# Edge sums on one core: smaller requests in more places between the tiles, leftover list and piece places through TensorE, third part merged while the second is split

## The chip, the core and the metric

The kernel runs on one core of a Trainium2 chip. The engines are TensorE (PE, with its weight loads listed apart as PEld), VectorE (DVE), ScalarE (ACT), GpSimd (POOL) and SyncE (SP). Each works through its own queue in order. The metric is the device time of one execution in microseconds. "Before" was run three times. A profile is one further execution.

## The reference

```python
def reference(x, src, dst, deg_inv, w_self, w_neigh):
    N = x.shape[0]
    nsum = _segment_sum(x[src], dst, N)
    h_neigh = nsum * deg_inv[:, None]
    return x @ w_self + h_neigh @ w_neigh
```

There are 12,500 nodes with 64 features each and 800,000 edges whose source and destination are drawn at random. For every destination the features of its sources are summed, scaled and multiplied by a 64x64 matrix; the node's own features through another matrix are added. Almost all of the work lies in bringing 800,000 edges into an order in which the sums can be made.

## The kernel before

**The order.** Every edge becomes a 32-bit key: a bucket (a block of 164 destinations with a block of 128 sources) and the two places inside the blocks. Each of the 128 partitions sorts 6,250 keys on DVE. The buckets are then dealt out in three parts of 128 rows, with 29, 20 and 10 buckets a row. For each part the places of 16 pieces in the sorted runs are counted (`find_rows`, ACT), the pieces are fetched by POOL and merged by DVE (lengths `LENA`), the rows are split once more among 8 (`split_rows`) and merged to the end (`LENB`). Then 128 keys around each bucket are fetched, decoded and turned (`change`). The edges beyond 128 in a bucket are the leftovers: `leftovers` picks them from the list `top`, brings two, four or seven rows together in `many`, picks again into `ltop`, and turns that list so that each column `lk` holds 128 leftover edges.

**The places.** `swap` turns counts that lie one way across the partitions into places that lie the other way: DVE subtracts (`st` or `stb`), DVE multiplies with a mask into `swapa`, one TensorE matmul writes `stp`, and DVE adds a base into the places `ixa` or `ixb`. POOL fetches by these. `split_rows` is run in one go of the generator as far as its ACT passes go (L530 to L534, eight sign passes with sums), then DVE's `stb` (L536), `swapa` (L487), `ixb` (L492), and POOL's eight fetches (L544), one a tile.

**The node stage.** `nodes` runs over the buckets in tiles of 8, some 945 tiles. For each 28 buckets SP loads a slab `slb` (L892) and DVE makes two one-hot tables, `ohs` (L894) and `ohd` (L899). For each tile PE selects the sources into `ct` (L925, 8 matmuls), ACT copies `ct` to `xg` (L935), and PE adds to `acc` (L1005, 16 matmuls of 64 rows, as 2 per bucket). Leftovers are fetched by POOL in columns of 128 (`lx`, `pick`, L956), spread by DVE (`ohl`, `spread`, L965) and added by PE (L973). PSUM has three buffers under the tag "ct"; `stp`, `po` and `fps` use the same ones.

**What sets the order.** The loop of `sums_and_merge` issues, after each tile, pieces of the other work. Merging of the second and third part is dealt out by a budget: `PACE` nanoseconds of estimated DVE time are added for each tile, and merge instructions are issued while the budget is above zero. `later_parts` is the one list from which this budget draws: the rest of the second part's `LENA` merges, its split, its `LENB` merges, and then the same for the third part. While a split waits (`"wait", 1` for each fetch, `"wait", 6` at the end), nothing is drawn. `leftovers` runs beside it and says by `yield` how many tiles to let pass:

```python
queue = nc.gpsimd if part else nc.scalar
queue.dma_start(self.tops[part], ...); yield 3
nc.vector.memset(many[:chk], 0.0)
queue.dma_start(many[...], self.tops[part]...); yield 8
...  # picks by DVE
queue.dma_start(self.lt[part]..., top); yield 3
queue.dma_start(k.bitcast(F32), ...lt turned...); yield 8
```

For the first part these four transfers are issued by ACT, for the others by POOL; the turn is done by writing `ltop` to DRAM and reading it across. Once the third part is turned (`self.changed`), DVE takes every other copy of `ct` (L933). After the last leftover list `check` (L1087) adds up counters; its one matmul `fps` follows DVE's sum `one` at once, and DVE reads `fps` at once.

## Time and profile before

| what | value |
|---|---|
| three runs | 1911.93, 1916.02, 1918.82 us (median 1916.02) |
| the profiled execution | 1898.32 us, span 1896.5 us, mean TensorE clock 0.973 |
| DVE busy | 1749.0 us (92%) |
| ACT busy | 1116.9 us (59%) |
| PE busy | 956.3 us (50%) |
| POOL busy | 569.8 us (30%) |
| DMA in the node stage, share of the 16 engines | 0.7 to 0.9 |

A row of the windows view gives a stretch of the span, its length, the busy time of each engine with the number of instructions, the mean granted TensorE clock and the share of the DMA engines. A row of the timeline gives the start, the time, the engine, the line, the operation, tiles and shapes, the count, and in brackets how long the engine stood idle before it and what ended that. Instructions of one kind that follow each other are one row with a count. The node stage begins at about 838 us.

### The profile page before, as it was taken

The page shows a single profiled execution, that of the slowest core. Times are in us where ns is not written, and L with a number is a line of the kernel's source. Part 1 is how long each engine was busy: PE and PEld are TensorE (multiplying, and loading weights), DVE is VectorE, ACT ScalarE, POOL GpSimd, SP SyncE. Part 2 cuts the span into 40 slices and gives each one's busy share as a digit, 9 for nine tenths or more (in the row PEclk, how much of TensorE's full clock was granted, in tenths as well). Part 3 has the DMA queues.
Part 4 walks back from the last instruction along what each step waited for, and adds up shares of the span by engine and source line. Part 5 has one row for each costly group of instructions (what it writes and reads, how often), then busy time and mean ns, then how long its engine had stood idle before and what let it go on. Part 6 is the DMA issues. An engine that isn't in the chain of part 4 may idle for free.

```text
span 1896.5 us, 54072 instructions
## 1 busy us (share of the span) xinstructions
PE 956.3 (50%) x23320; PEld 848.7 (45%) x23320; DVE 1749.0 (92%) x1773; ACT 1116.9 (59%) x1565; POOL 569.8 (30%) x440
## 2 busy tenths in 40 slices
PE   0052000000000000027799999897888899889996
PEld 0042000000000000016688888776777788778885
DVE  8999999999998999987899999999997999888985
ACT  7281000204001004338799999899889899968885
POOL 2000000055411100713435443573515224441341
PEclk9999999999999999998899999999998999989998
DMA  4353000022001100248798998987797899778994
GB/s 154 70 133 70 0 0 0 37 66 61 14 8 50 31 0 37 63 146 251 221 276 253 287 267 282 283 261 225 197 288 228 271 263 300 250 199 285 274 275 116
DMA packets 185332, 307.83 MB, mean 162 GB/s; under 512 B 136185, under 2 KB 141859, under 8 KB 184444
## 3 DMA queue, kind: packets, MB, share of 16 engines
q1 hardware_dynamic: 98268, 275.33, 44.5%
q0 software_dynamic: 78240, 28.72, 9.1%
q8 instruction: 184, 3.01, 0.6%
q10 hardware_dynamic: 8576, 0.24, 0.3%
q14 instruction: 64, 0.52, 0.1%
HBM read 277.29 MB, written 26.48 MB: 160 GB/s over the span
## 4 chain that ended last, share of the span: by engine, by line
DVE 21%; PE 18%; DMA 10%; issue 6%; ACT 5%; SPq 4%; POOL 2%; DVEq 0%; ACTq 0%; POOLq 0%
PE ct L925 10%; DMA slb<-sl 8%; DVE u L317 7%; PE acc L1005 7%; SPq L892 4%; DVE ohd L899 4%; DVE ohs L894 3%; ACT xg L935 3%; DVE u L351 2%; DMA lk<-lt 1%; POOL u L544 1%; PE acc L973 1%; PE po L1072 1%; POOL lx L956 1%; DVE ohl L965 1%
## 5 line engine op out<-in xcount | busy, mean ns | idle before, releaser
L935 ACT ACTIVATE xg<-ct 128x1024 f16<-128x1024 f32 x915 | 857.4, 1090 | 111.4 <-PE ct L925 79.3
L925 PE MATMUL ct<-xh,ohs 128*128 128x128 f16 x7546 | 530.6, 224 | 43.2 <-DVE ohs L894 22.2
L925 PEld LDWEIGHTS <-ohs 128*128 128x128 f16 x7546 | 453.9, 100 | 73.9 <-issue 27.9
L317 DVE TENSOR_TENSOR u<-u 128x1512 f32<-128x1512 f32 (+49 forms) x316 | 426.6, 1366 | 10.2 <-ACT u L301 6.2
L1005 PE MATMUL acc<-ohd,xg 64*128 64x82 f16 x15092 | 396.5, 201 | 41.2 <-ACT xg L935 16.3
L1005 PEld LDWEIGHTS <-xg 64*128 64x128 f16 x15092 | 325.4, 96 | 99.7 <-issue 30.6
L956 POOL DMA_INDIRECT lx<-xt,ls x127 | 241.1, 1899 | 427.4 <-PE acc L973 392.8
L899 DVE TENSOR_TENSOR ohd<-iota,dlT 128x2296 f16<-128x2296 bf16 x270 | 363.1, 1345 | 0.1
L894 DVE TENSOR_SCALAR ohs<-slb,pidx 128x3584 f16<-128x3584 bf16 x270 | 316.6, 1172 | 46.5 <-PE ct L925 24.2
L490 PE MATMUL stp<-cx,swapa 128*128 128x16 f32 (+1 forms) x12 | 3.5, 366 | 465.0 <-DVE swapa L487 465.0
L490 PEld LDWEIGHTS stp<-cx,swapa 128*128 128x128 f32 x12 | 3.0, 312 | 465.8 <-issue 301.4
L249 DVE TENSOR_TENSOR a<-b 128x1040 f32<-128x1040 f32 (+41 forms) x130 | 194.8, 1540 | 4.9 <-ACT b L251 1.7
L249 DVE TENSOR_TENSOR b<-a 128x1040 f32<-128x1040 f32 (+46 forms) x150 | 194.7, 1347 | 3.4 <-DVE a L249 0.5
L517 POOL DMA_INDIRECT u<-d,ixa x48 | 71.3, 1486 | 404.2 <-DVE ixa L492 396.9
L301 ACT ACTIVATE u<-u 128x256 f32<-128x256 f32 (+14 forms) x60 | 33.1, 625 | 174.1 <-DVE u L305 138.4
L695 POOL DMA_INDIRECT v<-d,ix x59 | 76.4, 1295 | 177.7 <-DVE ix L706 142.1
L251 ACT ACTIVATE b<-a 128x2 f32<-128x2 f32 (+31 forms) x41 | 16.0, 405 | 184.8 <-DVE a L249 167.4
L765 PE MATMUL tr<-idb,l 128*128 128x128 bf16 x59 | 8.0, 275 | 216.8 <-ACT l L759 216.8
L1081 POOL DMA_DIRECT2D out<-o x27 | 97.8, 3751 | 61.9 <-ACT o L1075 61.6
L765 PEld LDWEIGHTS <-l 128*128 128x128 bf16 x59 | 4.7, 119 | 219.2 <-POOL pad L415 171.0
L251 ACT ACTIVATE a<-b 128x1 f32<-128x1 f32 (+24 forms) x34 | 8.6, 259 | 118.8 <-DVE b L249 114.2
L305 DVE TENSOR_TENSOR u<-u 128x2016 f32<-128x2016 f32 (+11 forms) x40 | 62.0, 1564 | 15.2 <-DMA u<-da,ixb 8.2
(149 smaller groups left out, 784.4 us busy)
## 6 DMA issues: line engine op xcount, KB each, us to landing
slb<-sl SPq DMA_DIRECT2D x1076, 224.0 KB
xt<-xh SPq DMA_DIRECT2D x1, 3136.0 KB
out<-o POOLq DMA_DIRECT2D x25, 123.0 KB
own<-os SPq DMA_DIRECT2D x12, 256.0 KB
out<-os SPq DMA_DIRECT2D x12, 256.0 KB
rd<-dst SPq DMA_DIRECT2D x4, 521.0 KB
rs<-src SPq DMA_DIRECT2D x4, 521.0 KB
lx<-xt,ls POOLq DMA_INDIRECT x127
```

The source lines that it names most:

```text
L249: nc.vector.tensor_tensor(view(dst, lo + sh, [[st, g], [1, l]]), x, y, op=op)
L317: nc.vector.tensor_tensor(to, at(cur, ln + lo, n), at(cur, lo + k, n), op=op)
L517: nc.gpsimd.indirect_dma_start(out=u[:, i * w:(i + 1) * w], out_offset=None, in_=src, in_offset=bass.IndirectOffsetOnAxis(ap=self.start[pa ...
L695: self.nc.gpsimd.indirect_dma_start(out=self.v[:, k].bitcast(F32), out_offset=None, in_=flat(self.d2[part], 128 * PITCH2[part]), in_offset ...
L892: nc.sync.dma_start(b[j::4], bass.AP(tensor=src.tensor, offset=src.offset, ap=[[0, 32], [1, n * 128]]))
L894: nc.vector.tensor_scalar(s.rearrange("p c s -> p (c s)"), b, self.pidx[:, :1], None, op0=OP.is_equal)
L899: nc.vector.tensor_tensor(d, self.iota[:, None].to_broadcast(wide), ix, op=OP.is_equal)
L925: nc.tensor.matmul(ct[:, i * 128:(i + 1) * 128], cols[i][0], self.xh[:, (b0 + i) % NB].rearrange("p a f -> p (a f)"), start=True, stop=True)
L935: nc.scalar.activation(xg[:, :cnt * 128], ct[:, :cnt * 128], AF.Copy)
L956: nc.gpsimd.indirect_dma_start(out=x, out_offset=None, in_=self.xt, in_offset=bass.IndirectOffsetOnAxis(ap=self.left[p][1][:, c:c + 1].bit ...
L1005: nc.tensor.matmul(acc[h][:, db % OCT * HN:(db % OCT + 1) * HN], xg[r, i * 128:(i + 1) * 128], d[r], start=db % OCT == 0 and sb == 0, stop ...
L1081: nc.gpsimd.dma_start(out, o[:n, at], accum_op=OP.add)
```

## The change

**The places.** The subtraction and the addition move into the matmuls: the picking table is made negative, the constants are added up on the host into one table, and a second matmul with the identity adds that table in PSUM. DVE only makes `swapa`; ACT writes the places. In the node stage the steps are issued further apart: two of the eight ACT passes a tile, 4 tiles of pause, `swapa`, 6 tiles, the matmuls, 1 tile, the copy by ACT, a fetch a tile, and 5 tiles.

**The leftover list.** `many` is filled by POOL straight from `top` in on-chip memory, one transfer for each of the 2, 4 or 7 rows brought together; its clearing is done by POOL. The turn is a TensorE transpose `ltp` in a PSUM buffer of the tag "ct", copied by ACT. The tables `tops` and `lt` in DRAM are gone.

**The order of merging.** A stack of merge lists takes the place of `later_parts`. When a part's first merges are done, its split is queued beside the leftovers (to begin 6 tiles later); during the second part's split the budget goes to the third part's `LENA` merges, which have a buffer `u3` of their own. The budget is 270 and 275 instead of 260 and 300. Five leftover columns are held instead of four, they are spread up to 80 buckets ahead instead of 32, and `check` pauses 7 tiles ahead of its matmul and 6 behind it.

```diff
-PACE = (0, 260, 300)
+PACE = (0, 270, 275)
...
+HELD = 5
...
-          q[:, None] % NSUP == sup[None], q[:, None] % SUP == row[None]]
+          -(q[:, None] % NSUP == sup[None]).astype(np.float32), -(q[:, None] % SUP == row[None]).astype(np.float32)]
-        cx += [(q[:, None] % SUP * NSUP + sup[None]) * WIDE[p], (q[:, None] // SUP * SUP + row[None]) * PITCHA[p],
-               -(t - np.uint32(1)).view(np.float32), np.tile([n + lo - 1 for lo, n in WIN.wb[p]], (128, 1))]
+        at = np.array([n + lo - 1 for lo, n in WIN.wb[p]])
+        cx += [(q[:, None] % SUP * NSUP + sup[None]) * WIDE[p] + add[NSUP * p + q // SUP][:, None],
+               (q[:, None] // SUP * SUP + row[None]) * PITCHA[p] + at[q % SUP][:, None],
+               -(t - np.uint32(1)).view(np.float32)]
...
-    def swap(self, st, mps, mask, shape, pick, n, base, name):
+    def swap(self, acc, mps, mask, shape, pick, n, table, name):
         nc = self.nc
         a = self.keep.tile([128, 128], F32, name="swapa")
         nc.vector.tensor_tensor(a.rearrange("p (a b) -> p a b", a=view3[1]), src,
                                 mask.rearrange("p (a b) -> p a b", a=view3[1]), op=OP.mult)
+        yield 6
         ps = mps.tile([128, n], F32, name="stp", tag="ct", bufs=3)
-        nc.tensor.matmul(ps, a, pick, start=True, stop=True)
+        nc.tensor.matmul(ps, a, pick, start=True, stop=False)
+        nc.tensor.matmul(ps, self.idf, table, start=False, stop=True)
+        yield 1
         ix = self.keep.tile([128, n], U32, name=name)
-        nc.vector.scalar_tensor_tensor(ix, ps, 0.0, base, op0=OP.max, op1=OP.add)
-        return ix
+        nc.scalar.activation(ix, ps, AF.Copy)
+        self.places = ix
...
-        st = l1.tile([128, NSUP], F32, name=f"st{part}")
-        nc.vector.tensor_tensor(st, self.c1[:, 1, c0:c0 + NSUP], acc, op=OP.subtract)
-        self.start.append(self.swap(st, mps, self.cx[:, :128], ((NSUP, 1), (SUP, 0)),
-                                    self.cx[:, 256:256 + NSUP], NSUP, self.table(part, 0), f"ixa{part}"))
+        for _ in self.swap(acc, mps, self.cx[:, :128], ((NSUP, 1), (SUP, 0)), self.cx[:, 256:256 + NSUP], NSUP,
+                           self.table(part, 0), f"ixa{part}"):
+            pass
+        self.start.append(self.places)
...
-            yield i
-        st = self.keep.tile([128, SUP], F32, name=f"stb{part}")
-        nc.vector.tensor_tensor(st, self.table(part, 3), acc, op=OP.subtract)
-        yield SUP
-        ix = self.swap(st, mps, self.cx[:, 128:256], ((NSUP, 0), (SUP, 1)),
-                       self.cx[:, 256 + NSUP:256 + NSUP + SUP], SUP, self.table(part, 1), f"ixb{part}")
-        yield SUP
+            if i % 2:
+                yield 1
+        yield 4
+        for wait in self.swap(acc, mps, self.cx[:, 128:256], ((NSUP, 0), (SUP, 1)),
+                              self.cx[:, 256 + NSUP:256 + NSUP + SUP], SUP, self.table(part, 1), f"ixb{part}"):
+            yield wait
+        ix = self.places
         for j in range(SUP):
             self.pause(1)
-            yield SUP
+            yield 1
+        yield 5
...
-        queue = nc.gpsimd if part else nc.scalar
-        queue.dma_start(self.tops[part], self.top.rearrange("p j i -> p (j i)"))
-        yield 3
         many = pool.tile([max(CHK), max(g * (9 * c + 1) for g, c in zip(GRP, PCS))], F32, name="many")
-        nc.vector.memset(many[:chk], 0.0)
+        nc.gpsimd.memset(many[:chk], 0.0)
         many = many[:chk, :grp * n].rearrange("p (b i) -> p b i", b=grp)
-        full, rest = divmod(128, grp)
-        queue.dma_start(many[:full, :, :cand], self.tops[part][:full * grp].rearrange("(a b) i -> a b i", b=grp))
-        if rest:
-            queue.dma_start(many[full:chk, :rest, :cand], self.tops[part][full * grp:].unsqueeze(0))
+        found = self.top.rearrange("p j i -> p (j i)")
+        for b in range(grp):
+            nc.gpsimd.dma_start(many[:len(range(b, 128, grp)), b, :cand], found[b::grp])
         yield 8
...
-        yield 2
-        queue.dma_start(self.lt[part].rearrange("a (j i) -> a j i", i=8), top)
-        yield 3
+        yield 6
+        ps = self.mps.tile([128, chk], F32, name="ltp", tag="ct", bufs=3)
+        nc.tensor.transpose(ps, top.rearrange("p j i -> p (j i)"), self.idf[:chk, :chk])
+        yield 1
         k = pool.tile([128, chk], I32, name="lk")
-        src = self.lt[part]
-        queue.dma_start(k.bitcast(F32), bass.AP(tensor=src.tensor, offset=src.offset, ap=[[1, 128], [128, chk]]))
-        yield 8
+        nc.scalar.activation(k.bitcast(F32), ps, AF.Copy)
+        yield 5
...
-            if self.picked == len(done) or len([u for u in uses if u[5]]) >= 4:
+            if self.picked == len(done) or len([u for u in uses if u[5]]) >= HELD:
-                x = u[5] = pool.tile([128, 128], FH, name="lx", bufs=4)
+                x = u[5] = pool.tile([128, 128], FH, name="lx", bufs=HELD)
-            u[7] = pool.tile([128, 2, OCT * HN], FH, name="ohl", bufs=4)
+            u[7] = pool.tile([128, 2, OCT * HN], FH, name="ohl", bufs=HELD)
-            for u in uses[:4]:
-                if u[5] and not u[7] and len(done) >= u[6] + 10 and b0 + 32 >= (u[4] - 1) * NB:
+            for u in uses[:HELD]:
+                if u[5] and not u[7] and len(done) >= u[6] + 10 and b0 + 80 >= (u[4] - 1) * NB:
                     spread(u)
...
         nc.vector.tensor_reduce(one, self.cnt, axis=mybir.AxisListType.X, op=OP.add)
+        yield 7
         ps = mps.tile([1, 1], F32, name="fps", tag="ct", bufs=3)
         nc.tensor.matmul(ps, one, ones, start=True, stop=True)
+        yield 6
         nc.vector.tensor_scalar(self.flag, ps, float(E + 128 * 64 * (4 * n - sum(KPRS))), None, op0=OP.not_equal)
...
-        for dt in merge:
-            yield "merge", dt
-        for part, (u, w, pong) in ((1, (u1, x, u1)), (2, (u2, u1, u2))):
-            if part == 2:
-                for dt in self.merge_runs(LENA[2], u2, u1, NSUP):
-                    yield "merge", dt
-            for i in self.split_rows(part, u, w, mps, self.nc.gpsimd):
-                if i >= SUP:
-                    yield "wait", 1
-            yield "wait", 6
-            for dt in self.merge_runs(LENB[part], w, pong, SUP):
-                yield "merge", dt
-            self.rows[part] = w
-            yield "done", part
...
-        lefts = {0: [self.leftovers(0), 2]}
+        self.mps = mps
+        side = [[self.leftovers(0), 0]]
-        later = self.later_parts(merge, x, u1, u2, mps)
-        until = 0
+        home = {1: (u1, x, u1), 2: (u2, u1, u2)}
+        todo = [(merge, None)]
+        given, checked = 0, False
+
+        def split(part, n):
+            u, w, pong = home[part]
+            for wait in self.split_rows(part, u, w, mps, self.nc.gpsimd):
+                yield wait
+            todo.append((self.merge_runs(LENB[part], w, pong, SUP), part))
+
...
-                            self.check(fin, mps)
+                            side.append([self.check(fin, mps), 0])
...
-                        lefts[part] = [self.leftovers(part), 0]
+                        side.append([self.leftovers(part), n + 3])
             t += PACE[min(merging, 2)]
-            while t > 0 and later:
+            while t > 0 and todo:
+                dt = next(todo[-1][0], None)
+                if dt is not None:
+                    t -= dt
+                    continue
+                rows = todo.pop()[1]
+                if rows:
+                    self.rows[rows] = home[rows][1]
+                    merging += 1
                 else:
-                    merging += 1
+                    given += 1
+                    assert given == 1 or merging == 2
+                    side.append([split(given, n), n + 6])
+                    if given == 1:
+                        todo.append((self.merge_runs(LENA[2], u2, u3, NSUP), None))
+            t = min(t, 0)
+        assert checked
+        for job, _ in side:
+            for _ in job:
+                pass
```

The lines of the changed kernel are shifted by a few (L925 is L924, L935 is L934, L894 is L893, L317 is L319, L305 is L307, L544 is L546).

The first place is ACT from the start of the node stage to the second part's split (`junkb` are the sign passes, `tops`, `many`, `lt` and `lk` the first part's leftover list). Before:

```order
L935 ACTIVATE xg<-ct 128x1024 x3
L833 DMA tops_68<-top_1457 128x171
L935 ACTIVATE xg<-ct 128x1024 x3
L839 DMA many<-tops_68 64x2x171
L935 ACTIVATE xg<-ct 128x1024 x10
L855 DMA lt_71<-ltop 64x128
L935 ACTIVATE xg<-ct 128x1024 x3
L859 DMA lk<-lt_71 128x64x1
L935 ACTIVATE xg<-ct 128x1024 x8
L532 ACTIVATE junkb,accb_2485<-u,cx 128x10
L532 ACTIVATE junkb,accb_2485<-u,cx 128x103
L532 ACTIVATE junkb,accb_2485<-u,cx 128x141
```

Now:

```order
L934 ACTIVATE xg<-ct 128x1024 x16
L858 ACTIVATE lk<-ltp 128x64
L934 ACTIVATE xg<-ct 128x1024 x16
L534 ACTIVATE junkb,accb_2652<-u,cx 128x9
L534 ACTIVATE junkb,accb_2652<-u,cx 128x103
L934 ACTIVATE xg<-ct 128x1024
L534 ACTIVATE junkb,accb_2652<-u,cx 128x141
L534 ACTIVATE junkb,accb_2652<-u,cx 128x170
L934 ACTIVATE xg<-ct 128x1024
L534 ACTIVATE junkb,accb_2652<-u,cx 128x194
L534 ACTIVATE junkb,accb_2652<-u,cx 128x213
```

ACT issues no transfer there any more, and between two of the sign passes stands a tile's copy.

The second place is DVE from the places of the second part's split to the first merge behind it (L305, or L307 now, with 4x368). Before:

```order
L492 SCALAR_TENSOR_TENSOR ixb_2543<-stp,cx 128x8
L894 TENSOR_SCALAR ohs<-slb,pidx 128x3584
L899 TENSOR_TENSOR ohd<-iota,dlT 128x2296
L894 TENSOR_SCALAR ohs<-slb,pidx 128x3584
L899 TENSOR_TENSOR ohd<-iota,dlT 128x2296
L894 TENSOR_SCALAR ohs<-slb,pidx 128x3584
L899 TENSOR_TENSOR ohd<-iota,dlT 128x2296
L965 TENSOR_SCALAR ohl<-wide,lp_2482 128x2x82
L894 TENSOR_SCALAR ohs<-slb,pidx 128x3584
L899 TENSOR_TENSOR ohd<-iota,dlT 128x2296
L965 TENSOR_SCALAR ohl<-wide,lp_2482 128x2x164
L305 TENSOR_TENSOR u<-u 128x4x368
```

Now, the last rows ahead of that merge, which stands 28 rows behind `swapa` in DVE's order (the rows `u<-u 128x8x...` are third-part merges):

```order
L893 TENSOR_SCALAR ohs<-slb,pidx 128x3584
L898 TENSOR_TENSOR ohd<-iota,dlT 128x2296
L319 TENSOR_TENSOR u<-u 128x8x100
L964 TENSOR_SCALAR ohl<-wide,lp_2296 128x2x164
L893 TENSOR_SCALAR ohs<-slb,pidx 128x3584
L898 TENSOR_TENSOR ohd<-iota,dlT 128x2296
L964 TENSOR_SCALAR ohl<-wide,lp_2296 128x2x82
L319 TENSOR_TENSOR u<-u 128x8x104
L964 TENSOR_SCALAR ohl<-wide,lp_2296 128x2x82
L893 TENSOR_SCALAR ohs<-slb,pidx 128x3584
L898 TENSOR_TENSOR ohd<-iota,dlT 128x2296
L307 TENSOR_TENSOR u<-u 128x4x368
```

Third-part merges now stand where only one-hot tables stood. Before the last third-part merge there are 192 `ohs` instructions in the one order and 197 in the other, of 270.

The third place is POOL at the second part's split (`da` is the store of its rows). Before:

```order
L527 DMA da_66<-u 128x2412
L956 DMA lx<-xt,ls_2467 128x128
L544 DMA u<-da_66,ixb_2543 128x368
L415 MEMSET pad 128x100
L544 DMA u<-da_66,ixb_2543 128x368
L415 MEMSET pad 128x100
L956 DMA lx<-xt,ls_2467 128x128
```

Now:

```order
L836 MEMSET many 64x574
L840 DMA many<-top_1451 64x171 x2
L955 DMA lx<-xt,ls_2281 128x128 x5
L529 DMA da_66<-u 128x2412
L955 DMA lx<-xt,ls_2281 128x128 x6
L546 DMA u<-da_66,ixb_3135 128x368
L415 MEMSET pad 128x100
L546 DMA u<-da_66,ixb_3135 128x368
```

Eleven leftover columns are fetched ahead of the split's fetches, one among them; before it was one ahead and three among them.

57 lines of the change are left out of this document (21 added, 36 removed).

## The prediction

> **What bounds it now.** I read the windows view by stretches of the node stage first, once for all engines and once for line L925 alone (its matmuls divided by 8 are tiles), then each engine's waits in the timeline.
>
> ```profile
> 838.00:950.00 112.00, 82.09 (x1960) 73.27 (x1961) 88.44 (x125) 83.03 (x106) 37.34 (x34) 0.88 0.81 248
> 950.00:1210.00 260.00, 243.75 (x6354) 217.39 (x6353) 247.72 (x239) 252.48 (x305) 113.98 (x48) 0.99 0.91 274
> 1210.00:1410.00 200.00, 164.27 (x4048) 144.51 (x4047) 196.18 (x295) 176.82 (x241) 95.52 (x55) 0.96 0.83 245
> 1410.00:1470.00 60.00, 51.59 (x1243) 46.19 (x1242) 43.47 (x49) 54.90 (x80) 29.93 (x26) 0.89 0.81 238
> 1470.00:1610.00 140.00, 129.35 (x3320) 114.84 (x3312) 137.01 (x158) 132.52 (x169) 46.18 (x26) 0.98 0.89 277
> 1610.00:1690.00 80.00, 63.38 (x1498) 55.97 (x1496) 67.31 (x120) 61.71 (x85) 33.90 (x22) 0.89 0.73 219
> ```
>
> ```profile
> 838.00:950.00 112.00, 49.53 (x654) 42.65 (x655) 0.88 0.81 248
> 950.00:1210.00 260.00, 142.31 (x2084) 120.95 (x2083) 0.99 0.91 274
> 1210.00:1410.00 200.00, 94.27 (x1310) 79.76 (x1309) 0.96 0.83 245
> 1410.00:1470.00 60.00, 30.16 (x411) 25.81 (x408) 0.89 0.81 238
> 1470.00:1610.00 140.00, 74.82 (x1080) 63.52 (x1080) 0.98 0.89 277
> 1610.00:1690.00 80.00, 37.17 (x492) 32.21 (x492) 0.89 0.73 219
> ```
>
> The second stretch is undisturbed: 2084/8 = 260.5 tiles in 260 us, 0.998 us each, with PE, DVE and ACT all at 94 to 97%. There is no single bound, and a tile will not get much cheaper. Against that price the others lose time: the first has 81.8 tiles in 112 us, 30 us too long; 1210 to 1410 has 163.8 in 200, 37 too long; 1410 to 1470 has 51.4 in 60, 9 too long; 1470 to 1610 has 135 in 140, 5 too long; 1610 to 1690 has 61.5 in 80, 19 too long. But 1210 to 1410, the largest, has DVE at 196.18 of 200: real work (the second part's counting and decoding), which the change leaves. The first and fourth stretches have DVE idle for 23.6 and 16.5 us. Those are waits, and they have names:
>
> ```profile
> 853.74 1.01 PE L925 MATMUL ct<-xh,ohs 128*128 128x128 f16 x8 [5.22 <-ACT xg L935]
> 854.68 1.28 PE L1005 MATMUL acc<-ohd,xg 64*128 64x82 f16 x32
> 860.34 0.80 PE L1005 MATMUL acc<-ohd,xg 64*128 64x82 f16 x32
> 883.70 0.57 PE L490 MATMUL stp<-cx,swapa 128*128 128x8 f32 x2 [9.57 <-DVE swapa L487]
> 909.76 0.29 PE L973 MATMUL acc<-ohl,lx 128*128 128x82 f16 x2 [9.49 <-DVE ohl L965]
> 1426.29 0.57 PE L490 MATMUL stp<-cx,swapa 128*128 128x8 f32 x2 [6.10 <-DVE swapa L487]
> 1452.88 1.13 PE L925 MATMUL ct<-xh,ohs 128*128 128x128 f16 x16 [2.10 <-DVE ohs L894]
> 1453.94 1.28 PE L1005 MATMUL acc<-ohd,xg 64*128 64x82 f16 x32
> 1680.49 0.19 PE L1097 MATMUL fps<-ones,one 128*1 128x1 f32 x2 [4.05 <-DVE one L1095]
> ```
>
> ```profile
> 852.67 3.77 ACT L935 ACTIVATE xg<-ct 128x1024 f16<-128x1024 f32 x4 [6.27 <-DVE many L836]
> 880.43 0.20 DVE L863 TENSOR_SCALAR ls<-lk 128x64 int32<-128x64 int32 x1 [4.43 <-DMA lk<-lt]
> 905.52 1.69 DVE L305 TENSOR_TENSOR u<-u 128x1472 f32<-128x1472 f32 x1 [8.19 <-DMA u<-da,ixb]
> 1425.65 0.17 DVE L536 TENSOR_TENSOR stb<-cx,accb 128x8 f32<-128x8 f32 x1 [5.85 <-ACT junkb L532]
> 1448.89 1.93 DVE L305 TENSOR_TENSOR u<-u 128x816 f32<-128x816 f32 x2 [6.35 <-issue]
> ```
>
> The first PE stall is ACT held in its queue by the transfer that waits for DVE's clearing of `many`. The second is DVE standing for `lk`, the list turned through DRAM, with `stb` and `swapa` queued behind it. The third is DVE standing for the split's fetches at the first merge, with the `ohl` that PE needs queued behind. At 1426 DVE waits for eight sign passes in a row.
>
> **Part by part.** *Places, ahead of the node stage.*
>
> ```profile
> 390.91 0.17 DVE L508 TENSOR_TENSOR st<-c,acc 128x16 f32<-128x16 f32 x1
> 391.12 0.29 DVE L487 TENSOR_TENSOR swapa<-st,cx 128x128 f32<-128x128 f32 x1
> 392.18 0.17 DVE L492 SCALAR_TENSOR_TENSOR ixa<-stp,cx 128x16 uint32<-128x16 f32 x1 [0.77 <-PE stp L490]
> 392.27 2.38 DVE L249 TENSOR_TENSOR b<-a 128x1038 f32<-128x1038 f32 x2
> ```
>
> From 390.91 to 392.27 DVE spends 1.36 us; only `swapa`'s 0.29 stays. There DVE is the bound (the sort goes straight on behind), so each swap gives 1.07. Four lie ahead of 838 us: **-4.3**. The two-pass `stp` matmul here becomes two matmuls, some 0.4 us more ahead of POOL's fetches, hidden because DVE has other merges.
>
> *First stretch.* The three stalls named are 5.2 + 9.6 + 9.5 = 24.3 us of PE, and DVE's idle time is 23.6. All three causes go: no transfer on ACT, no DRAM turn, and third-part merges for DVE while the split runs. What stays is DVE's own 88.44 us. At the undisturbed stretch's density (247.72/260 = 0.953) that is 92.8 us, so 112 - 92.8 = 19.2; I take off 2 for slab waits at the start: **-17**. Bounds: nothing if each stall is replaced, 24.3 if all of it counts.
>
> *Third part's split.* The 6.1 us stall goes, since ACT's passes come two a tile. The wait at 1448.89 for the fetches has a cause that stays: POOL.
>
> ```profile
> 1427.81 1.27 POOL L544 DMA_INDIRECT u<-da,ixb  x1 [9.32 <-DVE ixb L492]
> 1443.72 0.95 POOL L544 DMA_INDIRECT u<-da,ixb  x1 [0.17 <-issue]
> 891.47 1.05 POOL L415 MEMSET pad<- 128x100 f32 x1
> POOL lx L956 <- PE acc L973: 392.8, 82, 13.3
> ```
>
> From the first fetch to the merge took 1448.89 - 1427.81 = 21.1 us; the new order leaves 13 tiles, 13 us, with fewer `lx` among the fetches. Of the 9 us lost I take **-6**; bounds 0 and 9. In these 35 tiles DVE has no merges at all, so it runs ahead and a wait of some us is covered by its one-hot tables.
>
> *Budget.* From 1210 to 1610 DVE is at 98%, so 25 ns less merging a tile is 25 ns less time: 299 tiles x 0.025 = 7.5. In the second stretch 10 ns more, on engines at 95%: 260 x 0.010 = 2.6 back. The same merges last 5 slabs or 17.5 tiles longer, at the undisturbed price those tiles have anyway: **-4.9**, bounds +2.6 and -7.5.
>
> *Check and clearing.* PE's 4.05 at 1680.49 goes, because the matmul comes 7 tiles behind DVE's sum: **-4**. DVE's clearing of `many` and the smaller swaps: **-1**. The leftover columns spread earlier cost DVE the same and move no bound where DVE is full.
>
> *What it adds.* Five copies by ACT in the node stage; the nearest row is L726's small ACT copy:
>
> ```profile
> L726 ACT ACTIVATE ix<-acc,c 128x1 uint32<-128x1 f32 x30 | 12.2, 407 | 0.0
> L839 POOL DMA_DIRECT2D many<-tops x2: 800/1122/1445, 1326.2 to 1650.2; - x2
> ```
>
> 5 x 0.41 = 2.0. `ltp`, `stp` and `fps` each keep one of three "ct" buffers for 1 to 6 tiles; with two left PE's fill still overlaps ACT's copy, so I take 1. POOL gets 13 transfers of `many` at 0.8 to 1.45 us: for the third part 7, 5.6 to 10.2 us, against a pause of 8 tiles. No cover lost if the lower, 2 us of DVE if the upper. Together **+3**, bounds +1 and +6.
>
> Sum: -4.3 - 17 - 6 - 4.9 - 4 - 1 + 3 = **-34.2 us** on the profiled execution's 1898.3, 1864.1. The runs' median lies 17.7 above that execution, so the forecast for the median is 1916.0 - 34.2 = **1882 us**.
>
> One rule speaks against clearing `many` on POOL: the Trainium skill (SBUF — State Buffer, Who interferes with whom) says that a GpSimd instruction and a DVE instruction in a two-port mode block each other for the whole instruction. The trace agrees that they meet: the 0.20 us clearing of `pad` took 1.05 at 891.47, beside an `ohs`, and it was POOL that waited. By the rule, with DVE as the loser, three clearings could cost DVE some 1.6 us in all (as long as DVE's own took), and the sum would be -32.6.
>
> Stalls also cost a slow restart: 32 matmuls of L1005 took 1.28 behind a stall against 0.80. The Trainium skill (TensorE: Matmul & The Clock Gate, Part 1) ties a slow clock to idle windows of about 3.4 us. By that the stall of 2.10 at 1452.88 would cost nothing, but the row behind it reads 1.28 too; here the measurement decides, and short stalls left over are not free.
>
> **Rivals.** (1) *The fetches are late again.* `ixb` no longer ties DVE to PE, so DVE may reach the first merge ahead of ACT's places. Fetches of 21 us against 13 tiles leave 8 us of standing at each split, as 8.19 and 6.35 now. For: the pause is no longer than before. Against: in the first split DVE is full and so late itself. Then the first stretch gives 9 instead of 17 and the split nothing: 1882 + 14 = 1896.
>
> (2) *More comes back.* All of DVE's idle time in the first, fourth and sixth stretch is 23.6 + 16.5 + 12.7 = 52.8; if all goes with the 4.3, 1859. For: a smoother PE keeps its clock (0.88 and 0.89 in these stretches against 0.99). Against: the sixth's is ACT's decoding.
>
> (3) *Slower: POOL's queue.* POOL works in order, an `lx` stands until PE has freed its buffer (392.8 us in 82 waits, longest 13.3), and six now stand between the store of the rows and the fetches. If the fetches end 42 us instead of 21 behind the places, DVE stands 42 - 13 = 29 us at each split. At the third part's split DVE stood from 1442.5 and PE ran dry at 1450.8, so some 8 us are covered by tables made ahead; 21 a split remain: 1882 + 2 x 21 = 1924. It decides from where it eats the 34 us, 17 a split, which is fetches of 13 + 8 + 17 = 38 us. Against: these `lx` were issued tiles earlier and are mostly done.
>
> (4) *The change does not do what it says*: DVE stays the bound, ACT at 252.48 of 260 takes what is freed, and only the 4.3 and the 4 remain: 1908.
>
> **Chances.** Forecast 0.55, (1) 0.19, (2) 0.13, (3) 0.07, (4) 0.06. A change of under 0.3%, 5.7 us, cannot be told from none. Faster: nearly all of the forecast and (2), most of (1), half of (4): 0.86. Same 0.07, slower 0.07. The range takes in (1) and (4) above and most of (2) below: 1857 to 1910.
>
> **What would show it.** Right: no PE stall above 4 us between 845 and 915; `lk` read without a DVE wait; the tile count from the stage's start to 112 us later at 95 or more instead of 81.8; no DVE wait on PE behind `swapa`; DVE at most 97% where the budget is 275. Wrong: an L307 wait of 6 us or more at 4x368 or 4x204; an L955 wait ahead of the fetches; DVE waiting for `many`; a TensorE clock under 0.95 in the first 100 us of the stage.

## The result and the profile after

The changed kernel took 1886.92 us (median of 4 runs, 1884.63 to 1890.86) against 1917.42 for the kernel before beside it: a ratio of 0.984, 95% interval 0.9801 to 0.988. The forecast was 1882. Run again on the chip listed as number 4 the ratio was 0.9824 (0.9798 to 0.985), 1889.98 against 1924.80 us, and on number 5 it was 0.9836 (0.9799 to 0.9873), 1871.43 against 1901.46. One run of the kernel before took 3553.18 us and is left out of the ratios. The gain is 30 to 35 us wherever it was measured.

The profiled executions alone would have told another tale: 1898.32 before and 1890.86 after, 7.5 us apart. The execution that the prediction was read from was quick for that kernel, and the one of the change was the slowest of its four runs. Another profile of the kernel before took 1909.56 us, and its runs on chip 4 centred on 1921 to 1925. So I compare profiles taken on one chip, 4: the kernel before at 1909.56 (span 1907.8) and the changed kernel at 1890.99 (span 1889.1). They differ by 18.7 us of span. That is about half of the 34.8 us between the medians there, because 1909.56 was the quickest of that kernel's ten runs; no profile shows where the other half lies.

The first view is the windows view of one line, the selecting matmuls of the node stage: start and end, length, PE's busy time in these matmuls with their number (8 make a tile), then clock, DMA share and GB/s. The kernel before:

```profile
834.00:940.00 106.00, 45.17 (x567) 0.82 0.81 239
940.00:1300.00 360.00, 187.94 (x2728) 0.99 0.91 271
1300.00:1400.00 100.00, 48.74 (x668) 0.95 0.74 221
1400.00:1460.00 60.00, 26.25 (x315) 0.83 0.69 209
1460.00:1600.00 140.00, 75.88 (x1117) 1.00 0.89 272
1600.00:1700.00 100.00, 46.72 (x612) 0.90 0.76 235
1700.00:1840.00 140.00, 76.84 (x1152) 1.00 0.92 281
```

The changed kernel, the same view:

```profile
834.00:940.00 106.00, 50.89 (x636) 0.85 0.82 261
940.00:1300.00 360.00, 187.85 (x2723) 0.99 0.90 268
1300.00:1400.00 100.00, 51.38 (x726) 0.95 0.80 240
1400.00:1460.00 60.00, 29.17 (x354) 0.83 0.79 238
1460.00:1600.00 140.00, 76.29 (x1120) 1.00 0.90 269
1600.00:1700.00 100.00, 45.75 (x621) 0.93 0.79 238
1700.00:1840.00 140.00, 74.85 (x1123) 1.00 0.89 269
```

Divide the differences by 8: the changed kernel is ahead by 8.6 tiles at 940, then -0.6, +7.3 between 1300 and 1400, +4.9 in the third part's split, +0.4, +1.1 and -3.6, together 18.0 tiles. At the 1.0 us that a tile costs undisturbed this is about the 18.7 us of span. Fixed windows compare somewhat different work, since the change runs ahead, and two executions of one kernel differ too. So here are two of the windows in the first pair of profiles, the kernel before:

```profile
1300.00:1400.00 100.00, 48.93 (x665) 0.93 0.77 224
1400.00:1460.00 60.00, 28.19 (x377) 0.89 0.80 233
```

The changed kernel:

```profile
1300.00:1400.00 100.00, 51.14 (x716) 0.95 0.79 237
1400.00:1460.00 60.00, 29.64 (x364) 0.86 0.79 239
```

In this pair the change is ahead by 8.0 tiles at 940 and wins 6.4 from 1300 to 1400, but it loses 1.6 from 1400 to 1460. The kernel before alone differs between its two profiles by 0.4 tiles from 1300 to 1400 and by 7.8 from 1400 to 1460. So two places of the gain are seen in both pairs: the start (with the lead brought into it), and the window with the second part's decoding and leftovers, which was not in the forecast. A gain at the third part's split is seen in one pair only, within the scatter.

The next rows are the first window for all engines (PE, PEld, DVE, ACT, POOL), on chip 4 again. The kernel before:

```profile
834.00:940.00 106.00, 74.55 (x1677) 64.50 (x1678) 78.28 (x116) 71.18 (x89) 30.60 (x31) 0.82 0.81 239
```

The changed kernel:

```profile
834.00:940.00 106.00, 85.08 (x1910) 73.90 (x1910) 90.30 (x129) 83.59 (x106) 40.06 (x34) 0.85 0.82 261
```

DVE works 12.0 us more in the same time. By its lines in this window, 6.4 us more went into one-hot tables (56.0 to 62.4) and 5.9 into merges (16.8 to 22.7). Then the waits. These are rows of the timeline of the first profile of the changed kernel (1890.86 us), with the wait ahead of each in brackets:

```profile
853.87 0.34 PE L855 MATMUL ltp<-idf,ltop 64*128 64x64 f32 x1 [4.36 <-DVE ltop L825]
918.82 1.69 DVE L307 TENSOR_TENSOR u<-u 128x1472 f32<-128x1472 f32 x1 [2.24 <-DMA lx<-xt,ls]
1346.13 1.03 PE L924 MATMUL ct<-xh,ohs 128*128 128x128 f16 x8 [3.87 <-DVE ohs L893]
1443.01 1.01 DVE L307 TENSOR_TENSOR u<-u 128x816 f32<-128x816 f32 x1 [1.34 <-DMA u<-da,ixb]
1677.12 0.26 PE L855 MATMUL ltp<-idf,ltop 19*128 19x19 f32 x1 [3.48 <-DVE ltop L825]
```

The stalls of 9.57 and 9.49 us are gone. DVE's stands at the splits' first merges have fallen from 8.19 and 6.35 to 2.24 and 1.34. (The row with 2.24 names an `lx`, which POOL fetches among the split's own fetches; the one with 6.35 named no transfer but "issue", the profile's word for time in which an engine waits for nothing that it shows.) But the list's turn on TensorE has brought two stalls of its own, 4.36 and 3.48, because the transpose stands in PE's queue until DVE has picked `ltop`.

The second profile of the kernel before corrects the starting point. Its waits of PE of 2 us or more between 840 and 932 are these two:

```profile
851.63 0.83 PE L925 MATMUL ct<-xh,ohs 128*128 128x128 f16 x8 [4.12 <-ACT xg L935]
881.63 0.57 PE L490 MATMUL stp<-cx,swapa 128*128 128x8 f32 x2 [9.79 <-DVE swapa L487]
```

The first two stalls named in the prediction are there again. The third, 9.49 us behind `ohl`, is not, and DVE does not stand at either of the splits' first merges (it stands 10.43 ahead of a table at 1447.74): the 9.49 belonged to one execution of the kernel before.

### The profile page after: what moved, and what is told of

It reads as the page before. It is cut to its first block, busy times and chain, and to the rows that moved or that the text cites. A ratio compares the mean times of both kernels' runs of the same rounds, so it can differ in the third digit from the quotient of the medians.

```text
span 1888.9 us, 54079 instructions
## 1 busy us (share of the span) xinstructions
PE 971.2 (51%) x23335; PEld 851.8 (45%) x23335; DVE 1742.4 (92%) x1754; ACT 1124.8 (60%) x1578; POOL 540.9 (29%) x447
## 4 chain that ended last, share of the span: by engine, by line
PE 28%; DVE 13%; issue 8%; ACT 7%; DMA 5%; SPq 2%; POOL 1%; another core or an unknown queue 0%; DVEq 0%; ACTq 0%; POOLq 0%
PE ct L924 15%; PE acc L1004 12%; DVE u L319 6%; DMA slb<-sl 5%; ACT xg L934 5%; SPq L891 2%; DVE u L353 2%; DVE ohs L893 2%; DVE ohd L898 1%; PE acc L972 1%; PE po L1071 1%; ACT u L303 1%; ACT junkb L534 0%; POOL out L1080 0%; POOL lx L955 0%
## 5 line engine op out<-in xcount | busy, mean ns | idle before, releaser
L934 ACT ACTIVATE xg<-ct 128x1024 f16<-128x1024 f32 x918 | 863.7, 1077 | 107.9 <-PE ct L924 82.5
L924 PE MATMUL ct<-xh,ohs 128*128 128x128 f16 x7546 | 535.2, 224 | 55.3 <-issue 20.2
L924 PEld LDWEIGHTS <-ohs 128*128 128x128 f16 x7546 | 452.4, 100 | 92.1 <-issue 49.9
L319 DVE TENSOR_TENSOR u<-u 128x1512 f32<-128x1512 f32 (+58 forms) x316 | 426.1, 1364 | 13.0 <-ACT u L303 9.2
L1004 PE MATMUL acc<-ohd,xg 64*128 64x82 f16 x15092 | 404.8, 202 | 58.1 <-issue 30.4
L1004 PEld LDWEIGHTS <-xg 64*128 64x128 f16 x15092 | 328.3, 96 | 121.5 <-issue 53.4
L893 DVE TENSOR_SCALAR ohs<-slb,pidx 128x3584 f16<-128x3584 bf16 x270 | 322.8, 1196 | 59.2 <-PE ct L924 36.9
L955 POOL DMA_INDIRECT lx<-xt,ls x127 | 213.5, 1681 | 473.0 <-PE acc L972 415.9
L307 DVE TENSOR_TENSOR u<-u 128x2016 f32<-128x2016 f32 (+11 forms) x40 | 62.0, 1563 | 4.0 <-DMA lx<-xt,ls 2.2
```

The lines of the kernel that those rows point to most:

```text
L307: nc.vector.tensor_tensor(at(oth, to, n), x, y, op=op)
L319: nc.vector.tensor_tensor(to, at(cur, ln + lo, n), at(cur, lo + k, n), op=op)
L893: nc.vector.tensor_scalar(s.rearrange("p c s -> p (c s)"), b, self.pidx[:, :1], None, op0=OP.is_equal)
L924: nc.tensor.matmul(ct[:, i * 128:(i + 1) * 128], cols[i][0], self.xh[:, (b0 + i) % NB].rearrange("p a f -> p (a f)"), start=True, stop=True)
L934: nc.scalar.activation(xg[:, :cnt * 128], ct[:, :cnt * 128], AF.Copy)
L955: nc.gpsimd.indirect_dma_start(out=x, out_offset=None, in_=self.xt, in_offset=bass.IndirectOffsetOnAxis(ap=self.left[p][1][:, c:c + 1].bit ...
```

## The experiments

Two theories stood at the start. **T**: a stall that goes gives about what it lasted, so the parts of the change add up to the whole. **R**: DVE, ACT and PE are all close to full, a lead won early is given back, and a part undone costs little. Each kernel ran in 5 rounds beside the kernel before, unless stated. Ratios are to that kernel, with the 95% interval. The chips differ by up to 23 us for the same kernel, so microseconds are compared only on one chip.

### The change again, and two parts undone (chip 4)

The changed kernel, unedited:

> The changed kernel again, unedited, as the yardstick for the runs beside it. The time of the runs fell by 30.5 us (1917.4 to 1886.9), the profiled executions differ by only 7.4 (1898.3 and 1890.9). Theory T (each stall that went gives about its term): the ratio to the kernel before stays at 0.984, 30 us, and the one profiled execution of the kernel before was 18 us luckier than its runs. Rival R (the engines' density is the limit, most of the lead is given back at the end): a ratio of 0.994 or more, some 8 to 11 us.

Measured: 1889.98 us against 1924.80, 0.9824 (0.9798 to 0.985). T's figure, not R's.

The leftover list by way of DRAM, as before:

```diff
+        queue = nc.gpsimd if part else nc.scalar
+        queue.dma_start(self.tops[part], ...)
-        nc.gpsimd.memset(many[:chk], 0.0)
+        nc.vector.memset(many[:chk], 0.0)
-        for b in range(grp):
-            nc.gpsimd.dma_start(many[..., b, :cand], found[b::grp])
+        queue.dma_start(many[...], self.tops[part]...)
...
-        nc.tensor.transpose(ps, top..., self.idf[:chk, :chk])
-        nc.scalar.activation(k.bitcast(F32), ps, AF.Copy)
+        queue.dma_start(self.lt[part]..., top)
+        queue.dma_start(k.bitcast(F32), ...lt turned...)
```

> The change with the leftover list handled as before: its columns spread and its list turned through transfers by way of DRAM, on ACT's queue in the second part and POOL's in the third, and many cleared by DVE. Theory T: the two PE stalls at 853.74 (5.22) and the one behind lk (9.57, DVE idle 4.43) come back, and a shorter one at the third part: 10 to 12 us slower than the change, 1897 to 1899, with a PE wait of 4 us or more between 845 and 915 and a DVE wait on the transfer of lk. Rival R: DVE, ACT and PE are each at 94 to 97% in the stretches behind, and a lead gained here is given back by 1700: at most 4 us slower, 1891 or less, though the stalls show.

Measured: 1903.95 us, 0.9896 (0.9869 to 0.9924), 14.0 us slower than the change, above T's 10 to 12 and far from R's 4. Its timeline:

```profile
874.17 0.20 DVE L868 TENSOR_SCALAR ls<-lk 128x64 int32<-128x64 int32 x1 [6.88 <-DMA lk<-lt]
879.37 1.03 PE L930 MATMUL ct<-xh,ohs 128*128 128x128 f16 x8 [7.29 <-DVE ohs L899]
1369.26 0.43 PE L978 MATMUL acc<-ohl,lx 128*128 128x164 f16 x2 [4.41 <-DVE ohl L970]
```

DVE stands 6.88 us for `lk`, and PE 7.29 behind it, as T said; the other stall that T expected, 5.22, is back as 2.14 only. But there is a second place: PE waits 4.41 at 1369 behind a leftover column of the second part. In its window from 1300 to 1400 it has 678 selecting matmuls, against 726 with the change and 668 before:

```profile
1300.00:1400.00 100.00, 48.08 (x678) 0.96 0.80 231
```

So 6.0 of the 7.3 tiles that the change wins there are gone. How many of them hang on the list alone is less sure. Two kernels described below turn the list as the change does and differ from it in the budget or in the order of merging; they have 692 and 700 matmuls there:

```profile
1300.00:1400.00 100.00, 49.57 (x692) 0.97 0.79 235
1300.00:1400.00 100.00, 51.27 (x700) 0.93 0.78 231
```

That the old handling costs time, 14.0 us, is shown. That it costs some tiles in this window is likely, 2 to 6 by these rows of single executions; which of its four transfers does it was not tried.

The split issued in one go, as before, but with the places still by TensorE and ACT:

```diff
-            if i % 2:
-                yield 1
-        yield 4
...
-            yield wait
+            pass
```

> The change with the split's sign passes, swap and places issued in one go, as before (the places still by TensorE and ACT). Theory T: DVE's stand of about 6 us at the third part's split comes back (5.85 before, now waits of 1 to 5 us in pieces), and so does the late fetch at the first merge: 5 to 7 us slower, 1892 to 1894. Rival R: DVE runs ahead in that stretch anyway and PE and ACT set the pace, so the same wait moves: within 2 us of the change.

Measured: 1900.61 us, 0.988 (0.985 to 0.991), 10.6 us slower. More than T's 5 to 7, and R is out. The late fetch that T expected at the first merge does not show in its timeline. Its PE rows show a stall at both splits:

```profile
877.71 0.57 PE L490 MATMUL stp<-cx,swapa 128*128 128x8 f32 x2 [5.74 <-DVE swapa L486]
1413.20 0.56 PE L490 MATMUL stp<-cx,swapa 128*128 128x8 f32 x2 [6.56 <-DVE swapa L486]
```

Third part's first merges behind the second part's split, and with it a last budget of 290:

```diff
-PACE = (0, 270, 275)
+PACE = (0, 270, 290)
...
+                    if rows == 1:
+                        todo.append((self.merge_runs(LENA[2], u2, u3, NSUP), None))
...
-                    if given == 1:
-                        todo.append((self.merge_runs(LENA[2], u2, u3, NSUP), None))
```

> The change with the third part's first merges put behind the second part's split instead of into it; the last budget of the pace is 290 instead of 275, since the order cannot be built at 275. The PE stall of 9.49 us that L965's ohl caused should come back. Theory T: 8 to 9 us slower for the stall, 4.5 us more for 15 units of budget on some 300 tiles at most (the run with that budget alone takes this off): 1895 to 1901. Rival R: DVE does the same merges later in a stretch in which it is the bound anyway, so the stall costs at most a third: 1890 to 1893.

Measured: 1883.35 us, 0.9795 (0.9765 to 0.9825), 6.6 us quicker than the change: the sign is against both theories. Five of its six runs lie below all six of the change, though the intervals of the ratios overlap. The PE stall did not come back; instead DVE stands 5.29 us at the split's first merge (913.02), and PE does not notice: no PE wait of 2 us or more lies between 876 and 925 there. So the early merges are not needed to be without the 9.49 us stall; but the second profile of the kernel before, which merges late too, is also without it, so nothing here shows that the change cured it. The spreading of leftover columns farther ahead (`HELD`, 80 buckets) was not undone in any run.

### The parts alone, and the budget (chip 4)

The kernel before, unedited, in 3 rounds (10 runs):

> The kernel before again, unedited, for a second profiled execution. The first took 1898.32 us, and fifteen runs since took 1911.93 to 1930.66. Theory T: this profile is an ordinary one of 1912 to 1930 us, and the 18 to 25 us by which the first was quicker sit in the node stage, at waits that the change removed (PE stalls longer than the 5.2, 9.6 and 9.5 us that the first one shows). Rival R: the difference lies ahead of the node stage, or is spread over all its tiles, and has nothing to do with the change.

Measured: 1920.63 us, 0.9982 (0.996 to 1.0003), as it must be; its profile took 1909.56. T was right in that the 11 us by which the first profile was quicker sit in the node stage, but not in that they sit at the waits that the change removes. They are in PE's busy time. The next rows are PE's windows from 834 to the end of the span: the kernel before in the profile of the prediction and in this one, then the change in its first profile, on chip 4 and on chip 5:

```profile
834.00:1896.50 1062.50, 911.96 (x23132) 0.95 0.84 253
834.00:1907.80 1073.80, 923.68 (x23132) 0.95 0.84 250
834.00:1888.90 1054.90, 925.06 (x23139) 0.96 0.85 254
834.00:1889.10 1055.10, 923.43 (x23139) 0.95 0.84 254
834.00:1869.10 1035.10, 910.96 (x23139) 0.96 0.86 258
```

For the same 23132 matmuls PE is busy 11.7 us longer in the second profile of the kernel before. The first profile of the change, too, has the longer busy time, and that is why the first pair lay only 7.5 us apart. On chip 4 the two kernels have the same busy time within 0.3 us, and the change is shorter by its waits and its earlier start.

By the windows of line L925 the second profile of the kernel before loses its tiles from 1400 to 1460 (39.4 against 47.1) and from 1600 to 1700 (76.5 against 81.6). There PE comes through in bursts of 3 to 5 matmuls though nothing it waits for is late:

```profile
1437.59 0.38 PE L925 MATMUL ct<-xh,ohs 128*128 128x128 f16 x4 [0.57 <-issue]
...
1443.29 0.38 PE L925 MATMUL ct<-xh,ohs 128*128 128x128 f16 x4 [1.06 <-issue]
...
1446.15 0.34 PE L1005 MATMUL acc<-ohd,xg 64*128 64x82 f16 x4 [1.17 <-issue]
```

Added over PE's timeline rows from 834 to 1870, waits of the kind "issue" come to 20.5 us in the first profile and 45.3 in this one. They do not lengthen the stage by that, since PE's other waits fall from 114 to 89.2, and the sum stays at 134 to 135 us. In the eight profiles taken on chip 4 the issue waits are 45 to 55, in the four on chips 5 and 6 29 to 37; the first profile of the change, whose chip is not recorded, has 53.4. On chip 4 they are 45.3 before and 48.8 after, while PE's other waits fall from 89.2 to 72.9: there the change does not make the issue waits.

The budget alone at 290:

```diff
-PACE = (0, 270, 275)
+PACE = (0, 270, 290)
```

> The change with nothing but the last budget at 290 instead of 275, beside the run in which the third part's first merges also moved and which came out 6.6 us quicker than the change (1883.35 against 1889.98). Theory T (the budget of 275 gives time, 25 ns a tile over 300 tiles for 25 units, and the early merges remove a stall): 4.5 us slower than the change, 1894 to 1895. Rival B (the budget was cut too far and the node stage gained from the wider one): 5 to 7 us quicker, 1883 to 1885, and the early merges are then worth nothing. Rival M (the early merges are themselves the loss): within 2 us of the change, 1888 to 1892.

Measured: 1893.33 us, 0.985 (0.9822 to 0.9878). Medians say 3.3 us slower than the change and ratios 5.0, near T's 4.5, but the interval holds zero too. Against the same budget with late merges the ratios are 0.9850 and 0.9795, so by these two runs the early merges cost some 10 us on this chip. Why is open: DVE stands idle for up to 12.95 us in the third part's split here, but for up to 9.29 with late merges too, and from 1400 to 1460 it is busy 39.69 and 37.93 us. The run at 280 further down points the other way.

Places by TensorE and ACT, in the kernel before:

```diff
-        st = l1.tile([128, NSUP], F32, name=f"st{part}")
-        nc.vector.tensor_tensor(st, self.c1[:, 1, c0:c0 + NSUP], acc, op=OP.subtract)
...
-        nc.tensor.matmul(ps, a, pick, start=True, stop=True)
-        nc.vector.scalar_tensor_tensor(ix, ps, 0.0, base, op0=OP.max, op1=OP.add)
+        nc.tensor.matmul(ps, a, pick, start=True, stop=False)
+        nc.tensor.matmul(ps, self.idf, table, start=False, stop=True)
+        nc.scalar.activation(ix, ps, AF.Copy)
```

> The kernel before with the places by TensorE and ACT alone: the table added by a second matmul, ACT's copy in place of DVE's two instructions, and the wait of 7 tiles in the swap. Theory T: 1.07 us for each of four swaps ahead of the node stage, 4.3, and a part of the 9.57 and 6.10 us stalls behind swapa, because DVE no longer waits for PE there: 5 to 9 us quicker than the kernel before, 1916 to 1920. Rival R: only the 4.3 us ahead of the node stage, 1920 to 1921; later fetches could take even that back.

Measured: 1917.81 us, 0.9966 (0.994 to 0.9991), 6.2 us quicker than the kernel before's 1923.97. The interval, 2 to 12 us, holds both T's figure and R's 4.3. The first selecting matmul starts at 835.14, where the kernel before has 838.40. Ahead of the node stage DVE goes on without a gap, from `swapa` at 391.27 to the sort's next instruction at 391.48.

The long stalls stay, because DVE is late with `swapa` for another reason (ahead of the first it stands 6.02 us for `lk`):

```profile
879.09 0.57 PE L491 MATMUL stp<-cx,swapa 128*128 128x8 f32 x2 [10.31 <-DVE swapa L487]
1433.39 0.59 PE L491 MATMUL stp<-cx,swapa 128*128 128x8 f32 x2 [5.61 <-DVE swapa L487]
```

The leftover list on TensorE, in the kernel before (the edit of the second experiment, the other way round):

> The kernel before with the leftover list turned by TensorE and copied by ACT, its columns spread by POOL without DRAM, and many cleared by POOL; nothing else. Undoing this in the changed kernel cost 14.0 us (1903.95 against 1889.98). Theory T, now that the parts seem to add up: 12 to 16 us quicker than the kernel before, 1909 to 1913. Rival R (the parts hide one another: with the split's stalls still there, the leftover's are covered by them): 6 us or less, 1919 or more.

Measured: 1912.60 us, 0.9946 (0.9916 to 0.9975), 11.4 us quicker, a little below T's 12 to 16; the interval, 5 to 16 us, just reaches R's 6. The stall ahead of `stp` is halved, since DVE no longer stands for `lk`, and the transpose has its own short one:

```profile
858.56 0.34 PE L852 MATMUL ltp<-idf,ltop 64*128 64x64 f32 x1 [2.44 <-DVE ltop L822]
877.99 0.57 PE L490 MATMUL stp<-cx,swapa 128*128 128x8 f32 x2 [5.31 <-DVE swapa L487]
```

Here its window from 1300 to 1400 has only 681 matmuls, 1.6 tiles more than before, and PE still waits 6.6 us behind `ohl` there (6.8 before). So the list alone does not win the second place; what else in the change it needs was not tried.

On chip 4 the parts then read, by medians: places 6.2, leftover list 14.0 undone or 11.4 alone, spacing 10.6, together 28 to 31 of the 34.8 us. What is left, 4 to 7, is for the order of merging, the budget and the check. Each part is uncertain by 5 us or more either way. So the parts add up as T said as far as they can be resolved, and R, by which they cost little, does not stand for the list and the spacing; the order of merging fits neither.

### Third part's split, and a search for a better kernel (chip 6)

These three ran beside a kernel before of 1905.34 us. The spacing undone for the third part alone:

```diff
-            if i % 2:
+            if i % 2 and part == 1:
                 yield 1
-        yield 4
+        if part == 1:
+            yield 4
...
+            if part == 1:
                 yield wait
```

> The change with the split's sign passes, swap and places issued in one go for the third part alone; the second part's split keeps its new spacing. Undoing the spacing in both splits cost 10.6 us (1900.61 against 1889.98). The prediction put 6 us on the third part's split and, for the second, part of 17. Theory T (the third part's split holds the larger share, since DVE stands 6 us for the last sign pass there in every profile of the kernel before, and PE with it): ratio to the kernel before 0.987, 7 to 9 us slower than the change. Rival H (each split pays for its own stall, 5.74 and 6.56 us of PE in the run without spacing): ratio 0.985, 5 us slower. Rival E (the earlier split pays, because its delay pushes the second part's merges): within 2 us of the change, 0.982 to 0.983.

Measured: 1876.46 us, 0.9858 (0.9834 to 0.9882). The interval holds T's 0.987 and H's 0.985; E's 0.982 to 0.983 lies just below it.

Late merges with a budget of 280 (the edit of the kernel with 290, with that number):

> The change with the third part's first merges behind the second part's row merges, where the kernel before had them, and a last budget of 280 (275 cannot be built in that order). At 290 this was 1883.35 us against 1889.98 for the change and 1893.33 for the change with 290: ratios 0.9795, 0.9824 and 0.9850. Theory M (the early merges cost about 10 us in the changed kernel, and the budget gives about 0.33 us a unit): 3.3 us quicker than at 290, ratio 0.978, 1880. Rival N (what was seen at 290 is one lucky order of the tiles): ratio 0.981 to 0.984, 1887 to 1893.

Measured: 1882.18 us, 0.9892 (0.9867 to 0.9918). M expected 0.978; even N's range is missed on the high side.

The same with the leftover pick cut up:

```diff
-        self.pieces(many, grp * n, top, one)
         for j in range(one):
             w = view(many, j, ...)
+            nc.vector.max(out=top[:, j, :8], in_=w)
             nc.vector.scalar_tensor_tensor(w, w, top[:, j, 7:8], w, ...)
+            if j % 4 == 3:
+                yield 1
...
-        yield 6
+        yield 8
```

> The same order and budget (third part's merges late, 280), and the leftover list's pick by DVE cut into pieces: each maximum with its masking together, a pause of one tile after every four, and eight tiles instead of six ahead of the list's turn on TensorE. In the changed kernel PE stands 4.4, 3.9 and 3.5 us around this pick (at 853.87, 1346.13 and 1677.12). Theory T (a stall that goes gives its term): 8 to 11 us less than the same kernel without it. Rival R (DVE has the same work, and only the 4.4 at the start of the stage, where nothing is behind, counts): 2 to 4 us less.

Measured: 1887.75 us, 0.9918 (0.9892 to 0.9945), 5.6 us slower than without it by the medians, with intervals that overlap. Without it the stalls at the transpose were 3.90, 4.51 and 3.21; the longest:

```profile
1324.31 0.31 PE L855 MATMUL ltp<-idf,ltop 32*128 32x32 f32 x1 [4.51 <-DVE ltop L825]
```

They went, and others came. DVE has the same picks to do, and is late with tables or leftover columns instead:

```profile
857.66 1.03 PE L926 MATMUL ct<-xh,ohs 128*128 128x128 f16 x8 [6.05 <-DVE ohs L895]
1362.43 0.43 PE L974 MATMUL acc<-ohl,lx 128*128 128x164 f16 x2 [5.43 <-DVE ohl L966]
```

Here neither theory's gain came. The likely reading is that a stall is worth its length only if its cause is a wait; if its cause is DVE's own work, moving the wait gains nothing.

### The change a third time (chip 5)

> The changed kernel a third time, unedited, since the last three kernels ran beside a kernel before of 1905.34 us, 19 us quicker than in the earlier runs (1924.80 and 1923.97), so that their ratios (0.9858, 0.9892, 0.9918) may not be laid beside 0.9824. Theory T (the ratio of the change carries over from chip to chip): 0.980 to 0.985 again, whatever the kernel before takes; then the third part's spacing is worth 0.34% (6.5 us), and the late merges at 280, with or without the pick in pieces, lose to the change. Rival C (the change wins less where the kernel before is quicker): 0.987 or more if the kernel before is near 1905, and then the three say nothing against the change.

Measured: 1871.43 us against 1901.46, 0.9836 (0.9799 to 0.9873). T: the ratio carries over. So no kernel tried is shown to beat the change. The late merges at 280 lie at 0.9892 against 0.9836, with intervals that overlap; at 290 they were ahead on chip 4. Whether they are better or worse stays open, and so does the share of the third part's spacing (0.9858 against 0.9836 is within the intervals).

This profile holds one more finding. DVE stood at the first merge of both splits, as long as the first rival had said (the first row names again an `lx` among the fetches):

```profile
918.18 1.69 DVE L307 TENSOR_TENSOR u<-u 128x1472 f32<-128x1472 f32 x1 [9.21 <-DMA lx<-xt,ls]
1435.40 1.01 DVE L307 TENSOR_TENSOR u<-u 128x816 f32<-128x816 f32 x1 [7.17 <-DMA u<-da,ixb]
```

PE's waits behind them were 3.79 and 2.54 us:

```profile
920.99 1.83 PE L924 MATMUL ct<-xh,ohs 128*128 128x128 f16 x16 [3.79 <-DVE ohs L893]
1437.53 1.03 PE L924 MATMUL ct<-xh,ohs 128*128 128x128 f16 x8 [2.54 <-DVE ohs L893]
```

## Why the prediction was right, and where it was not

The forecast was 34.2 us off the median; the runs gave 30.5, and 34.8 and 30.0 on chips 4 and 5. The whole was right, but two terms were wrong in ways that cancel, and that they cancel is luck. The account by places also covers only the 18.7 us between the two profiles of chip 4.

**Places, -4.3: right.** The first selecting matmul starts at 838.4 and 839.6 in the two profiles of the kernel before and at 835.1 and 835.5 in the first two of the change, 3 to 4.5 us earlier, and at 835.14 with this part alone. Alone, the part gave 6.2 us with an interval that holds 4.3.

**First stretch, -17: mis-sized.** The named stalls went, and 8.6 tiles of lead stand at 940 (8.0 in the first pair). Some 3.3 of these are the places' lead (835.1 against 838.4), so about 5 us were won there in the profiles of chip 4. One reason is that the third stall, 9.49 of the 24.3 us, was read from a single execution; the second profile of the kernel before has only 4.12 and 9.79. Another is that I turned all of DVE's freed time into tiles. But of the 12.0 us by which DVE's busy time rose in the stretch 5.9 are merges: the third part's, which I had called upon as cover at no cost, are work that DVE does in the place of tables. And the term had no entry for the transpose: I charged a held buffer, not the 4.36 us in which PE stands for DVE's pick.

**"1210 to 1410 ... real work, which the change leaves": the step that failed.** This stretch holds the second part's leftover list. In the stretch as it was named the change has 166.5 and 168.5 tiles in its two profiles where the kernel before has 163.8 and 165.0, some 3 more; in the window from 1300 to 1400 it is 6.4 and 7.3, since the change, being ahead, has its third part's split already at 1410. With the list's old handling 6.0 of the 7.3 are gone again, but only 1.5 of the 168.5. DVE at 196.18 of 200 did look full. But PE stood behind leftover columns that came late: 7.7 and 6.8 us for `ohl` from 1300 to 1400 in the two profiles of the kernel before, and none in the change. I had costed the list where its wait was named, in the first part, and not the second time it runs. That the list is the cause here is in part argued, since alone it brought only 1.6 tiles.

**Third part's split, -6: the cause right, the size not shown.** With both spacings undone PE stands 6.56 at `stp` again. From 1400 to 1460 the change has 4.9 tiles more on chip 4 and 1.6 fewer in the first pair, and the two profiles of the kernel before differ by 7.8. Its share of the 10.6 us for both splits could not be told apart. And the wait of 6.35 that I read as one for the fetches is put down to "issue" in its row.

**Budget, -4.9: not refuted, not shown.** 15 of the 25 units cost 3.3 us by medians and 5.0 by ratios, within the uncertainty. DVE's 98%, from which I took the price, leave out the split's stretch, where it was busy 43.47 of 60.

**Check, -4: the stall went, the gain did not come.** No row shows PE waiting for the check's sum any more. But the third part's list now stalls PE 3.48 us close by, and from 1600 to 1840 the change has 2.5 tiles fewer than the kernel before on the same chip. The terms for the clearing, -1, and for what the change adds, +3, are too small to be seen in any run.

**Rivals.** (1) came true in its mechanism on chip 5, with fetches late by 9.21 and 7.17 against the 8 that it had, and false in its price: the ratio there was 0.9836. PE felt 3.79 and 2.54; that tables made ahead covered the rest is my reading. So the sign I named for a wrong prediction, a wait of 6 us or more at that merge, is none. (3), with POOL's queue, did not come: in the change's first profile POOL stands six times for PE between the rows' store and the second part's fetches, 16.2 us in all, but the first fetch starts at 898.60, 0.7 us behind the places (897.86). (2) was not reached on any chip, and (4) is out, since the gain exceeds it. Of the other signs, `lk` is read without a wait and `swapa` no longer has a wait on PE behind it; the 95 tiles in the first 112 us were not reached (716 and 684 matmuls from the first one on in the change's first two profiles, 89.5 and 85.5 tiles), one stall in the first stretch stayed above 4 us, DVE was at 99.56% from 1300 to 1400 on chip 4, and the clock in the first 100 us was 0.91 rather than 0.95.

**The offset.** Adding the difference between median and profile, 17.7 us, to the sum was right, but its meaning was unknown. It now has one in part: PE's busy time in the node stage, 912.0 us in that execution, 923.7 in the second one of the same kernel and 925.1 in the change's first. That the first profile came from a quick chip would fit; the chip is not recorded, and it stays a guess.

## What to carry to other kernels

When a helper runs several times, cost the edit at each of its runs, not only where a long wait names it; a full engine in that stretch is no proof that nothing can be won. Price a stall by its cause: here waits for a transfer or for a place in a queue could be removed, while a wait for DVE's own work came back under another name. Take a second profile of the kernel before first: one of three named stalls was not in it. And before laying one profile against another, see whether they differ in something that the change does not set, such as PE's busy time for the same matmuls.

## What the runs showed of the hardware

**PE's busy time for the same matmuls differed by about 12 us.** In the node stage it was 920 to 929 us in the eight profiles of chip 4, with issue waits of 45 to 55, and 910 to 916 in the four of chips 5 and 6, with issue waits of 29 to 37. The one kernel profiled on both sides, the change, has 923.43 on chip 4 and 910.96 on chip 5. The medians of the kernel before go the same way: 1920.63 to 1924.80 on chip 4, 1905.34 and 1901.46 on the others. What holds PE there was not tried.

**The mean clock says nothing of the time here.** A window ahead of the node stage, first profile of the kernel before and then the second:

```profile
400.00:834.00 434.00, 6.28 (x35) 4.02 (x35) 412.84 (x400) 87.44 (x232) 132.27 (x164) 1.00 0.12 37
```

```profile
400.00:834.00 434.00, 6.27 (x35) 4.02 (x35) 412.82 (x401) 87.40 (x232) 130.51 (x160) 0.50 0.12 38
```

With PE nearly idle the clock reads 1.00 in one execution and 0.50 in the other, DVE does the same work in the same time, and in the node stage both read 0.95. The changed kernel took 1890.99 us at a mean of 0.794 and 1888.97 at 0.978. The Trainium skill (TensorE: Matmul & The Clock Gate, Part 1) says that half rate is what an idle TensorE falls back to after a window of about 3.4 us. The second execution agrees with 0.50; the first, with 6.28 us of matmuls in 434 and a clock of 1.00, does not.
